# An attention and gated-MLP kernel: a second block's scores in pairs, and the lower halves of weights on another engine

## The chip, the cores and the metric

The kernel runs on one core of a Trainium2 chip. Its engines work side by side, each through its own queue of instructions: TensorE (PE; its weight loads are listed as PEld), VectorE (DVE), ScalarE (ACT), GpSimd (POOL) and SyncE (SP), which issues the DMAs. The metric is the device time in microseconds (us) of one execution.

## The reference

Local attention with a few global tokens, and a gated feed-forward layer behind it, all in float32:

```python
scores = scale * q @ k.T            # 4 batches, 8 heads, 768 tokens, head size 64
keep = (pos_k < 8) | ((rel >= 0) & (rel < 96))
a = softmax(where(keep, scores - slope[h] * dist, -1e9))
x = (a @ v), heads side by side     # 3072 tokens x 512
gate = 1 / (1 + exp(-(x @ w_gate)))            # 512 x 1536
out = (gate * (x @ w_val)) @ w_out             # 1536 x 512
```

## The kernel before, in words

**Tiles.** The 3072 tokens are cut into eight blocks of three tiles of 128 tokens (`TB`, `NB` = 384). Heads are taken in pairs, so a block has 4 pairs x 3 tiles = 12 items `(s, t)`. For an item the kernel computes the scores of both heads against a window of 256 keys (`WIN`: 96 before, 32 global slots, the 128 of the tile itself), adds a table of biases and takes the minimum of the negated row on VectorE (L406, in one instruction that also writes the minimum), the exponential with its sum on ScalarE (L419), the normalisation on VectorE (L438), the transposes (L452) and the product with v (L502). The result x of a block lies transposed, split into an upper half xh (rounded to the fast float form of TensorE) and a lower half xl, the remainder.

**Feed-forward.** The 1536 hidden columns are cut into 12 slices f. `ff_in` (L554) computes the gate (`ps_g`) and the value (`ps_u`) of a slice: for each, four chunks of 128 model columns times three products (w1l with xh, w1h with xl, w1h with xh). `ff_out` (L588) multiplies by the output slice and adds into three banks `ps_o`, again as three products with w2h and w2l. For the first six slices of the first block (`UNSPLIT`) the output slice is not split, and one product in full float32 stands in place of three. `ff_out` of a slice is issued after `ff_in` of the next one.

**Weights.** They arrive as 64 bit floats. Within the first block they are converted, in steps that `conv_step` (L241) advances: `conv_load` asks for the raw words two steps ahead; `conv_a` (L182) makes bits and exponent parts on ScalarE and VectorE; `conv_b` (L208) puts them together on VectorE; `conv_c` (L230) copies gate and value of a slice to the upper half w1h on ScalarE (128x1024) and takes the difference to the lower half w1l with two GpSimd subtractions of 128x512. w1h and w1l of all slices then stay in SBUF. The output slices stay unsplit as `w2f`; `split_w2` (L221, with `split`, L216) makes w2h on ScalarE and w2l on GpSimd anew for each slice and block, into one buffer each.

**Order of the work.** The first block's attention stands before everything else. The second block's attention (`PAIR` = 1) is spread over the twelve slices of the first block; later blocks' attention over the slices of the block before, with a split form and with transposes by DMA. A list of events gives each step its slice and one of four places in it (L632 to 654): 0 before `ff_in`, 1 between gate and value, 2 after `ff_in`, 3 after `ff_out`. For the second block an item's scores ("S") stood at place 0 of slice `k * 10 // 12`, its transposes ("T") at place 1 of the next slice, and the values ("V") of a pair of heads behind the last T. The third S of a pair of heads also asks for the loads of a later pair (`ready_step`, `load_step`, L289). Within this, a scheduler of the language orders the instructions of each engine by a model of their times and by priorities; `issue_after` (L62) fixes single places in the order without a wait.

**Banks.** The second block's scores used two PSUM banks, `ps_s` and `ps_v`, one for each head of an item, each holding 256 of 512 columns; the next item used the same two (`bank`, L351; `scores`, L359). The scores are matmuls in full float32 on half the rows of the array each, the second head's first (L371 to 378).

Of the kernel before, what the change touches and what calls it, by code (L numbers as in the profile page):

```python
# [8 lines left out]
F32 = mybir.dt.float32  # L9
# [6 lines left out]
ALU = mybir.AluOpType  # L16
# [3 lines left out]
P = 128  # L20
# [8 lines left out]
def attn_moe_kernel(ctx, tc, qT, kT, v, n_global, n_local, wg, wv, wo, out, B, H, S, D):  # L29
# [31 lines left out]

    def issue_after(later, earlier):  # L62
        tc.add_manual_dep(
            later.ins,
            earlier.ins.name,
            mybir.DependencyInfo(mybir.DependencyClass.NoSync, mybir.DependencyReason.DATA),
            reason="issue order",
        )
# [146 lines left out]

    def split(hi, lo, w):  # L216
        ins = nc.scalar.activation(hi, w, AF.Copy)  # L217
        sub(nc.gpsimd, lo, w, hi)
        return ins

    def split_w2(f, last=False):  # L221
        if last:
            hi, lo = (mpool.tile([P, DM], F32R, name="work", tag="work", bufs=WORKB) for _ in range(2))
        else:
            hi = w2pool.tile([P, DM], F32R, name="w2h")
            lo = w2pool.tile([P, DM], F32R, name="w2l")
        issue_after(split(hi, lo, w2f[f].bitcast(F32)), last_gate[-1])
        w2[0] = (f, hi, lo)

    def conv_c(j):  # L230
        c = conv[j]
        if c["i"] == 0:
            hi, lo = (t[c["f"]].rearrange("p i c n -> p (i c n)") for t in (w1h, w1l))
            w = c["bits"].bitcast(F32)
            nc.scalar.activation(hi, w, AF.Copy)
            for part in (slice(0, CW), slice(CW, 2 * CW)):
                sub(nc.gpsimd, lo[:, part], w[:, part], hi[:, part])
# [113 lines left out]
    def bank(*names):  # L351
# [5 lines left out]
        return pool.tile([P, 4 * P], F32, name=name)  # L357

    def scores(bi, s, t):  # L359
        b, t0, nt = blocks[bi]  # L360
# [5 lines left out]
        if bi <= PAIR:  # L366

            ps = [bank(*(("ps_s", "ps_g", "ps_u", "ps_o1") if bi < PAIR else ("ps_s", "ps_v"))) for _ in range(2)]

            lead = None  # L370
            for j in (1, 0):  # L371
                hd = slice(j * D, (j + 1) * D)
                ins = nc.tensor.matmul(
                    ps[j][:, :w], st["qr"][hd, 0, qc], st["kr"][hd, k0:k0 + w], start=True, stop=True
                )
                if lead is not None:
                    issue_after(ins, lead)
                lead = ins
            last_pe[:] = [lead]
            if (bi, s, t) == (0, 0, 1):  # L380
# [134 lines left out]
    def pair_out(bi, s, av, st):  # L515
# [3 lines left out]
        if bi < PAIR:  # L519
# [17 lines left out]
            x = mpool.tile([P, NB], F32, name="hh", tag="hh")  # L537
            nc.vector.tensor_tensor(x[:, :n], av[:, :n], rs[:, :n], op=ALU.mult)
            if s < NPAIR - 1:
# [14 lines left out]
    def ff_in(bi, f, mid=None):  # L554
# [4 lines left out]
        for i in range(2):  # L559
            ps = ps_gv.tile([P, NB], F32, name=("ps_g", "ps_u")[i])  # L560
            k = 0
            for c in range(NC):
                for wt, xt in ((w1l, xh), (w1h, xl), (w1h, xh)):
                    nc.tensor.matmul(  # L564
                        ps[:, :n], wt[f][:, i, c], xt[:, c, :n], start=(k == 0), stop=(k == 3 * NC - 1)
                    )
                    k += 1
            pss.append(ps)
            if i == 0:
                a = mpool.tile([P, NB], F32, name="work", tag="work", bufs=WORKB)  # L570
# [62 lines left out]
    for bi, (b, t0, nt) in enumerate(blocks):  # L633
# [5 lines left out]
        else:  # L639

            w = ((bi - 1) * NF - (LEAD + 1 if bi > PAIR + 1 else 0), bi * NF - LEAD - 1)
        for k, (s, t) in enumerate(items):
            u = w[0] + k * (w[1] - w[0]) // len(items)

# [5 lines left out]
            if t == nt - 1:  # L650
                after, kind = (2, 2) if bi < PAIR else (1, 1) if bi == PAIR else (2, 3)
                events.append((u + after * lag, kind, "V", bi, s, t))
# [51 lines left out]
    for u, (bi, f) in enumerate(seq):  # L704
# [36 lines left out]
        if bi >= PAIR or f >= UNSPLIT:  # L741
            split_w2(f, u == len(seq) - 1)
        prev = (bi, f)
# [152 lines left out]
```

## Time and profile before

| | us |
|---|---|
| median of 3 runs | 738.48 |
| lowest and highest | 736.40, 741.03 |
| the profiled execution | 736.18 |
| its span, first to last instruction | 734.4 |
| TensorE busy | 718.1 |
| VectorE busy | 498.8 |
| ScalarE busy | 420.2 |
| GpSimd busy | 219.4 |

The profile's times count from the span's start. A busy TensorE contains matmuls that overlap their neighbours, as they are pipelined; how fast it goes is read from the starts of one matmul and the next. "Idle before" names the instruction whose end released an engine after a wait.

### The profile page before, as it was taken

Reading aid. Unit: us, or ns where it says so; the run is one execution under the profiler, and the core shown is the slowest. Engines: PE = TensorE matmul, PEld = TensorE weight load, DVE = VectorE, ACT = ScalarE, POOL = GpSimd, SP = SyncE. Lnnn points to the kernel's source line nnn. Section 1 sums busy time; section 2 is a strip of 40 time slices with the busy share of each in tenths; the row PEclk is TensorE's granted clock in tenths of the full one; section 3 lists DMA queues with packets and bytes.
Section 4 is the critical chain, followed back from the end, with each engine's and each line's share of the span. In section 5 each row is a group of like instructions: output and inputs, shape, how many; then the busy total and the mean of one; then the engine's idle time right before and its main releaser. Section 6 shows DMA issues by size and latency. Waiting matters only on the chain. (4 is left out here: it accounts for less than half of the span.)

```text
span 734.4 us, 12477 instructions
## 1 busy us (share of the span) xinstructions
PE 718.1 (98%) x4403; PEld 653.0 (89%) x4403; DVE 498.8 (68%) x1303; ACT 420.2 (57%) x948; POOL 219.4 (30%) x166
## 2 busy tenths in 40 slices
PE   7999999999999999999999999999999999999996
PEld 5667788999889999999999999999999999999996
DVE  7889799668877777686777868666786877321111
ACT  5789887656565555566456655655555664332222
POOL 5424345422231323223132332313233231221222
PEclk9999999999999999999999999999999999999999
DMA  8969662624437353433435442343435224010001
GB/s 249 275 194 274 189 199 59 167 61 81 106 79 159 85 106 71 100 103 68 79 80 121 110 106 63 65 122 74 96 81 110 72 47 83 16 45 1 1 0 46
DMA packets 136866, 74.27 MB, mean 101 GB/s; under 512 B 87136, under 2 KB 129120, under 8 KB 136800
## 3 DMA queue, kind: packets, MB, share of 16 engines
q1 hardware_dynamic: 136800, 73.43, 40.1%
q8 instruction: 36, 0.59, 0.3%
q14 instruction: 30, 0.25, 0.1%
HBM read 49.81 MB, written 6.29 MB: 76 GB/s over the span
## 5 line engine op out<-in xcount | busy, mean ns | idle before, releaser
L180 POOL TENSOR_TENSOR w2l<-w2f,w2h 128x512 fp32r<-128x512 f32 x89 | 122.5, 1377 | 372.8 <-ACT w2h L217 359.1
L581 DVE SCALAR_TENSOR_TENSOR work<-work,ps_u 128x384 f32<-128x384 f32 x90 | 49.8, 553 | 127.1 <-PE ps_u L564 122.1
L564 PE MATMUL ps_g<-xh,w1l 128*128 128x384 f32 x384 | 131.1, 341 | 1.0 <-ACT work L572 1.0
L564 PE MATMUL ps_u<-xh,w1l 128*128 128x384 f32 x384 | 130.9, 341 | 0.1
L564 PE MATMUL ps_g<-xl,w1h 128*128 128x384 f32 x384 | 129.6, 337 | 0.7 <-DVE xl L545 0.7
L564 PE MATMUL ps_g<-xh,w1h 128*128 128x384 f32 x384 | 129.4, 337 | 0.0
L564 PE MATMUL ps_u<-xh,w1h 128*128 128x384 f32 x384 | 129.3, 337 | 0.0
L564 PE MATMUL ps_u<-xl,w1h 128*128 128x384 f32 x384 | 129.2, 336 | 0.0
L584 ACT ACTIVATE hh<-work 128x384 fp32r<-128x384 f32 x90 | 46.9, 521 | 131.3 <-DVE work L581 131.1
L419 ACT ACTIVATE work<-work,nms 128x256 f32<-128x256 f32 (+1 forms) x192 | 92.0, 481 | 25.8 <-DVE nms L406 25.4
L604 PE MATMUL ps_o<-w2l,hh 128*128 128x512 f32 x267 | 104.9, 393 | 0.6 <-POOL w2l L180 0.5
L604 PE MATMUL ps_o<-w2h,hh 128*128 128x512 f32 x267 | 104.1, 390 | 0.0
L604 PE MATMUL ps_o<-w2h,hl 128*128 128x512 f32 x267 | 103.1, 389 | 0.0
L180 DVE TENSOR_TENSOR hl<-work,hh 128x384 fp32r<-128x384 f32 x90 | 79.6, 884 | 23.4 <-ACT hh L584 23.2
L217 ACT ACTIVATE w2h<-w2f 128x512 fp32r<-128x512 f32 x89 | 56.0, 630 | 52.3 <-PE ps_o L604 51.0
L564 PEld LDWEIGHTS ps_g<-xh,w1l 128*128 128x128 f32 x384 | 72.2, 188 | 5.1 <-issue 2.3
L564 PEld LDWEIGHTS ps_u<-xh,w1l 128*128 128x128 f32 x384 | 72.1, 188 | 3.9 <-issue 1.2
L564 PEld LDWEIGHTS ps_g<-xl,w1h 128*128 128x128 f32 x384 | 72.2, 188 | 2.6 <-DVE xl L545 1.1
L564 PEld LDWEIGHTS ps_u<-xl,w1h 128*128 128x128 f32 x384 | 72.2, 188 | 1.0
L438 DVE TENSOR_SCALAR work<-work,rc 128x256 f32<-128x256 f32 (+1 forms) x168 | 71.4, 464 | 2.0
L564 PEld LDWEIGHTS ps_g<-xh,w1h 128*128 128x128 f32 x384 | 72.2, 188 | 0.5 <-issue 0.2
L564 PEld LDWEIGHTS ps_u<-xh,w1h 128*128 128x128 f32 x384 | 72.2, 188 | 0.0
(133 smaller groups left out, 1170.0 us busy)
## 6 DMA issues: line engine op xcount, KB each, us to landing
qr<-in_qT SPq DMA_DIRECT2D x56, 192.0 KB, 3.3
kr<-in_kT SPq DMA_DIRECT2D x32, 192.0 KB, 2.7
v<-in_v SPq DMA_DIRECT2D x32, 192.0 KB, 3.6
raw<-in_w_gate SPq DMA_DIRECT2D x12, 512.0 KB, 4.3
raw<-in_w_val SPq DMA_DIRECT2D x12, 512.0 KB, 5.6
raw<-in_w_out SPq DMA_DIRECT2D x12, 512.0 KB, 3.8
out<-ost SPq DMA_DIRECT2D x24, 256.0 KB, 2.2
v<-in_v SPq DMA_DIRECT2D x16, 144.0 KB, 3.8
```

What stands on the lines that cost most here:

```text
L180: eng.tensor_tensor(out, a, b, op=ALU.subtract)
L217: ins = nc.scalar.activation(hi, w, AF.Copy)
L419: ins = nc.scalar.activation(sb[:, j, :w], sb[:, j, :w], AF.Exp, scale=-1.0, bias=nm[:, j:j + 1], accum_out=sm[:, j:j + 1])
L438: nc.vector.tensor_scalar(sb[:, j, :w], sb[:, j, :w], rc[:, j:j + 1], None, op0=ALU.mult)
L564: nc.tensor.matmul(ps[:, :n], wt[f][:, i, c], xt[:, c, :n], start=(k == 0), stop=(k == 3 * NC - 1))
L581: nc.vector.scalar_tensor_tensor(a[:, :n], a[:, :n], 1.0, pss[1][:, :n], op0=ALU.add, op1=ALU.mult)
L584: nc.scalar.activation(hh[:, :n], a[:, :n], AF.Copy)
L604: ins = nc.tensor.matmul(outs[bi][t], ht[:, t * P:(t + 1) * P], wt, start=(f == 0 and k == 0), stop=(f == NF - 1 and k == len(parts) - 1),)
```

## The change

- `pair_scores` computes the scores of items into two banks. For the second block it takes two items: the first item's 256 columns lie in the left half of each bank, the second's in the right half. The matmuls are issued at a priority raised by 400, in their place behind the last feed-forward matmul written so far (`last_out`, which `ff_in` of the first block now notes too), and wait with a semaphore for the last minimum (`last_min`) and for the product of the first block's last pair of heads (`last_av`), which had the bank before.
- `twin_scores` is called by the first item of a pair and keeps the second's banks for its own call.
- The events of the second block are counted in quarters of a slice: both S of a pair at one place, every 6 or 7 quarters; T four quarters after S for the first item and six for the second; V one quarter after a pair of heads' last T.
- `conv_c` takes w1l of slices 1 to 11 with one VectorE subtraction of 128x1024 instead of two on GpSimd; slice 0 keeps them.
- `split` and `split_w2` get an engine: w2l of the first block (slices 6 to 11) goes to VectorE, the later blocks' stays on GpSimd.

```diff
-    def issue_after(later, earlier):
+    def issue_after(later, earlier, kind=mybir.DependencyClass.NoSync):
...
-    def split(hi, lo, w):
+    def split(hi, lo, w, eng):
         ins = nc.scalar.activation(hi, w, AF.Copy)
-        sub(nc.gpsimd, lo, w, hi)
+        sub(eng, lo, w, hi)
         return ins
...
             nc.scalar.activation(hi, w, AF.Copy)
+            if c["f"]:
+                sub(nc.vector, lo, w, hi)
+                return
             for part in (slice(0, CW), slice(CW, 2 * CW)):
                 sub(nc.gpsimd, lo[:, part], w[:, part], hi[:, part])
...
+    def pair_scores(bi, items):
+
+        names = ("ps_s", "ps_g", "ps_u", "ps_o1") if bi < PAIR else ("ps_s", "ps_v")
+        banks = [bank(*names) for _ in range(2)]
+        free = [] if bi < PAIR else [last_av[-1], last_min[-1]]
+        turn = [] if bi < PAIR else last_out[-1:]
+        lead = None
+        out = []
+        with tc.high_priority(offset=0 if bi < PAIR else 400):
+            for i, (s, t) in enumerate(items):
+                st = steps[bi, s]
+                w = P if blocks[bi][1] + t == 0 else WIN
+                qc = slice(t * P, (t + 1) * P)
+                k0 = t * SLOT + WIN - w
+                ps = [b[:, i * WIN:i * WIN + w] for b in banks]
+                for j in (1, 0):
+                    hd = slice(j * D, (j + 1) * D)
+                    ins = nc.tensor.matmul(ps[j], st["qr"][hd, 0, qc], st["kr"][hd, k0:k0 + w], start=True, stop=True)
+                    for before in free:
+                        issue_after(ins, before, mybir.DependencyClass.Sync)
+                    if bi < PAIR and lead is not None:
+                        issue_after(ins, lead)
+                    for before in turn:
+                        issue_after(ins, before)
+                    lead = ins
+                out.append(ps)
+        last_pe[:] = [lead]
+        return out
+
+    def twin_scores(bi, s, t):
+        nt = blocks[bi][2]
+        s2, t2 = divmod(s * nt + t + 1, nt)
+        ps, steps[bi, s2]["ps", t2] = pair_scores(bi, [(s, t), (s2, t2)])
+        return ps
...
+            ps = st.pop(("ps", t), None)
+            if ps is None:
+                ps = pair_scores(bi, [(s, t)])[0] if bi < PAIR else twin_scores(bi, s, t)
...
+            if bi < PAIR:
+                last_out[:] = [ins]
...
+            if bi == PAIR:
+                at = 4 * (k - k % 2) * w[1] // len(items)
+                turned = at + 4 + 2 * (k % 2)
+                events.append((*divmod(at, 4), "S", bi, s, t))
+                events.append((*divmod(turned, 4), "T", bi, s, t))
+                if t == nt - 1:
+                    events.append((*divmod(turned + 1, 4), "V", bi, s, t))
+                continue
...
-            split_w2(f, u == len(seq) - 1)
+            split_w2(f, u == len(seq) - 1, nc.vector if bi < PAIR else nc.gpsimd)
```

## Rows read from the trace of the kernel before

**Rows 1.** The page: busy tenths in 40 equal slices of the span.

```profile
PE   7999999999999999999999999999999999999996
...
DVE  7889799668877777686777868666786877321111
```

**Rows 2.** Busy us (instructions) in three stretches; then granted clock, DMA share, GB/s.

```profile
core 0: us, PE busy (x) PEld busy (x) DVE busy (x) ACT busy (x) POOL busy (x), PEclk, DMA share, GB/s
36.00:130.00 94.00, 91.33 (x510) 71.59 (x510) 83.50 (x160) 78.83 (x150) 39.50 (x27) 1.00 0.61 186
130.00:200.00 70.00, 68.18 (x423) 63.29 (x422) 50.84 (x155) 43.14 (x106) 22.44 (x15) 1.00 0.42 99
200.00:720.00 520.00, 519.92 (x3175) 487.96 (x3174) 334.51 (x882) 272.92 (x622) 136.43 (x93) 1.00 0.34 76
```

**Rows 3.** TensorE's timeline: start, us, instruction, count, [idle before <-releaser].

```profile
36.28 0.48 PE L373 MATMUL ps_v<-kr,qr 64*128 64x256 f32 x1
...
36.93 0.44 PE L564 MATMUL ps_g<-xh,w1l 128*128 128x384 f32 x1
...
38.28 0.44 PE L564 MATMUL ps_g<-xl,w1h 128*128 128x384 f32 x1 [0.74 <-DVE xl L545]
38.56 0.34 PE L564 MATMUL ps_g<-xh,w1h 128*128 128x384 f32 x1
38.74 0.34 PE L564 MATMUL ps_u<-xl,w1h 128*128 128x384 f32 x1
...
39.18 0.48 PE L373 MATMUL ps_v<-kr,qr 64*128 64x256 f32 x1
...
40.46 0.42 PE L564 MATMUL ps_g<-xh,w1l 128*128 128x384 f32 x1 [0.57 <-ACT work L572]
...
58.73 0.48 PE L373 MATMUL ps_v<-kr,qr 64*128 64x256 f32 x1 [0.84 <-DVE nms L406]
...
198.81 0.51 PE L387 MATMUL ps_s<-ks,qs 128*128 128x256 f32 x2 [1.20 <-DVE ks L180]
```

**Rows 4.** VectorE's groups from 36 to 130 us: busy us, mean ns | idle before.

```profile
L438 DVE TENSOR_SCALAR work<-work,rc 128x256 f32<-128x256 f32 x24 | 12.3, 551 | 0.2
L214 DVE SCALAR_TENSOR_TENSOR w2f<-top,w2f 128x512 int16<-128x512 int16 x11 | 11.9, 1085 | 1.9 <-ACT w2f L192 1.5
L206 DVE SCALAR_TENSOR_TENSOR top<-raw,neg 128x512 int16<-128x512 int16 x11 | 11.6, 1054 | 0.2
...
L180 DVE TENSOR_TENSOR hl<-work,hh 128x384 fp32r<-128x384 f32 x5 | 4.9, 988 | 0.6 <-ACT hh L584 0.6
...
L545 DVE TENSOR_TENSOR xl<-hh,xh 128x384 fp32r<-128x384 f32 x1 | 1.3, 1321 | 0.8 <-ACT xh L544 0.8
```

**Rows 5.** VectorE's timeline, single instructions: start, us, instruction.

```profile
42.05 0.68 DVE L206 SCALAR_TENSOR_TENSOR top<-raw,neg 128x512 int16<-128x512 int16 x1
...
42.84 0.74 DVE L214 SCALAR_TENSOR_TENSOR w2f<-top,w2f 128x512 int16<-128x512 int16 x1
...
43.65 0.35 DVE L438 TENSOR_SCALAR work<-work,rc 128x256 f32<-128x256 f32 x1
...
63.13 1.84 DVE L214 SCALAR_TENSOR_TENSOR w2f<-top,w2f 128x512 int16<-128x512 int16 x1
...
114.01 0.55 DVE L180 TENSOR_TENSOR hl<-work,hh 128x384 fp32r<-128x384 f32 x1
...
198.00 0.76 DVE L180 TENSOR_TENSOR ks<-kr,ks 64x576 fp32r<-64x576 f32 x1
```

**Rows 6.** Waits of SP's queue, 30 to 130 us: total, times, longest.

```profile
SPq L324 <- PE ps_t L502: 5.2, 2, 4.8
```

**Rows 7.** GpSimd's groups from 36 to 130 us, columns as in rows 4.

```profile
L180 POOL TENSOR_TENSOR w1l<-bits,w1h 128x512 fp32r<-128x512 f32 x22 | 31.7, 1461 | 40.6 <-ACT w1h L235 40.4
L180 POOL TENSOR_TENSOR w2l<-w2f,w2h 128x512 fp32r<-128x512 f32 x5 | 8.4, 1687 | 17.0 <-ACT w2h L217 10.4 <-ACT sm L432 6.5
```

**Rows 8.** GpSimd's timeline from 62 to 67 us.

```profile
63.05 3.02 POOL L180 TENSOR_TENSOR w1l<-bits,w1h 128x512 fp32r<-128x512 f32 x2 [3.93 <-ACT w1h L235]
```

**Rows 9.** ScalarE's copy to w1h, its group from 36 to 130 us.

```profile
L235 ACT ACTIVATE w1h<-bits 128x1024 fp32r<-128x1024 f32 x11 | 11.7, 1063 | 9.4 <-DVE bits L212 9.3
```

More of the change, by code (lines that the diff above doesn't have):

```diff
@@ L65, in issue_after @@
             earlier.ins.name,
-            mybir.DependencyInfo(mybir.DependencyClass.NoSync, mybir.DependencyReason.DATA),
+            mybir.DependencyInfo(kind, mybir.DependencyReason.DATA),
             reason="issue order",
@@ L214, in conv_b, with split_w2 @@
             nc.vector.scalar_tensor_tensor(top, c.pop("top"), 8.0, top, op0=ALU.mult, op1=ALU.add)
-    def split(hi, lo, w):
+    def split(hi, lo, w, eng):
         ins = nc.scalar.activation(hi, w, AF.Copy)
-        sub(nc.gpsimd, lo, w, hi)
+        sub(eng, lo, w, hi)
         return ins
-    def split_w2(f, last=False):
+    def split_w2(f, last=False, eng=nc.gpsimd):
         if last:
@@ L226, in split_w2 @@
             lo = w2pool.tile([P, DM], F32R, name="w2l")
-        issue_after(split(hi, lo, w2f[f].bitcast(F32)), last_gate[-1])
+        issue_after(split(hi, lo, w2f[f].bitcast(F32), eng), last_gate[-1])
         w2[0] = (f, hi, lo)
@@ L357, in bank @@
         return pool.tile([P, 4 * P], F32, name=name)
+    last_av = []
+    def pair_scores(bi, items):
[30 more added lines that the diff above has]
+        return ps
     def scores(bi, s, t):
@@ L366, in scores @@
         if bi <= PAIR:
[L368 to L379, printed above, removed]
+            ps = st.pop(("ps", t), None)
+            if ps is None:
+                ps = pair_scores(bi, [(s, t)])[0] if bi < PAIR else twin_scores(bi, s, t)
             if (bi, s, t) == (0, 0, 1):
@@ L537, in pair_out @@
             x = mpool.tile([P, NB], F32, name="hh", tag="hh")
-            nc.vector.tensor_tensor(x[:, :n], av[:, :n], rs[:, :n], op=ALU.mult)
+            last_av[:] = [nc.vector.tensor_tensor(x[:, :n], av[:, :n], rs[:, :n], op=ALU.mult)]
             if s < NPAIR - 1:
@@ L563, in ff_in @@
                 for wt, xt in ((w1l, xh), (w1h, xl), (w1h, xh)):
-                    nc.tensor.matmul(
+                    ins = nc.tensor.matmul(
                         ps[:, :n], wt[f][:, i, c], xt[:, c, :n], start=(k == 0), stop=(k == 3 * NC - 1)
@@ L650, in attn_moe_kernel @@
             if t == nt - 1:
-                after, kind = (2, 2) if bi < PAIR else (1, 1) if bi == PAIR else (2, 3)
+                after, kind = (2, 2) if bi < PAIR else (2, 3)
                 events.append((u + after * lag, kind, "V", bi, s, t))
```

## The prediction

> **What bounds the kernel now.** First the page's slices [rows 1]: TensorE's digit is 9 in all of them but the first and the last, while VectorE stands at 7 to 9 only in the first third and at 6 to 7 later. Then the stretches that the change touches [rows 2]. From 36 to 130 us (the first block's slices, with the second block's attention between them) TensorE is busy for 91.33 of 94.00 us, so 2.67 us pass without a matmul; from 130 to 200 us 1.82 us; in the 520 us after that 0.08. The granted clock is 1.00 in all three, the 2.4 GHz level. So the time is the sum of what TensorE has to do plus small holes. Whoever wants to gain has to close holes before 200 us (4.5 us in these two stretches) or take TensorE work away; whoever loses has to open new ones. VectorE, with 83.50 of 94.00 us, has 10.5 us free in the first block's stretch, less than any engine but TensorE.
>
> Third, the order of TensorE's instructions with what ended its holes [rows 3]. At 36.28 us stand the first item's scores, then a gate matmul; 0.74 us of hole in front of 38.28 wait for xl, the lower half of the first block's activations, from VectorE. At 39.18 come the second item's scores; 0.57 us in front of 40.46 wait for ScalarE's tanh. In front of the scores at 58.73 lie 0.84 us, which wait for VectorE's minimum of the item before: their bank was still to be read. These three are 2.15 of the 2.67 us.
>
> The profiled execution took 736.18 us: 734.4 of span and 1.78 around it. The median of the runs shown is 738.48, 2.30 above. I do the sums on 736.18 and add 2.30 at the end.
>
> **The change part by part.**
>
> *Scores in pairs.* The 24 score matmuls stay; only their places change. An item's scores take 0.65 us of TensorE's order (36.28 to 36.93 [rows 3]), so a second item right behind the first costs the same again. What a group of scores costs beside that is the return: the first gate matmul behind a hole or a change of form takes 0.28 us to the next start (38.28 to 38.56), the one after it 0.18 (38.56 to 38.74). Six groups fewer save 6 x 0.10 = 0.6 us. That transposes which now stand beside scores lose this neighbour can eat it: bounds 0 and 0.6; I take 0.6, since transposes and scores of other pairs also come to stand together.
>
> The second gain is the wait for the bank. Before, both banks belong to one item, and the next item comes less than a slice later; this cost 0.84 us at 58.73. Now a pair comes every 1.5 to 1.75 slices, some 13 us at 94 us for about twelve slices, and four minima have to be taken in that time. The hole goes: 0.84 us. The new wait (semaphores of the last minimum and of the product of the first block's last pair) holds what is behind the scores on TensorE's queue, which is the next gate or output matmuls, and with them all that reads these banks; with 13 us of room I price it at nothing. Its bounds: nothing, and 0.84 us for each of the six pairs, 5.0 us, if VectorE lags each time as it did once.
>
> The third is the start. The second item's scores now stand behind the first's, at about 36.9 us, in front of a gate that waits for xl until 38.28 in any case. So their 0.65 us fall into the hole of 0.74, and the separate group at 39.18 goes. Besides, that xl took 1321 ns [rows 4] where the same form took 0.55 us later [rows 5], beside a GpSimd subtraction that now goes away. Either closes the hole; both together don't give it twice: 0.74 us. The 0.57 us in front of 40.46 wait for ScalarE, which nothing here speeds up: they stay.
>
> Transposes come a slice or one and a half after their scores, values a quarter later; each keeps at least the slack it had, so 0. The loads of q, k and v for a later pair of heads hang on a third item's scores and move by two or three quarters of a slice either way. They stand on SP's queue in front of weight loads, and the load of v waits there until the values before it have been computed: 4.8 us at the longest now [rows 6]. Two of these waits grow by two quarters, some 4 us. I take 0, since the weights are asked for two steps ahead of their use; bounds 0 and 8 us, both uncovered.
>
> The dependency kind, the note of the last input matmul and the priority of 400 issue no instruction; they only fix the places counted above: 0.
>
> *Lower halves on VectorE.* Removed from GpSimd: 22 subtractions of 128x512 for w1l, 1461 ns each, and six for w2l (five of them in this stretch), 1687 ns each [rows 7]. Slice 0 keeps its two. GpSimd was busy for 39.50 of 94.00 us [rows 2], so its relief by itself is worth nothing. Added on VectorE: 11 subtractions of 128x1024 and 6 of 128x512. No row of before has that form with 1024 columns. Undisturbed, 384 columns took 0.55 us and 576 took 0.76 [rows 5], 1.09 ns a column; hence an estimate of 1.25 us for 1024 and 0.69 for 512, together 13.8 + 4.1 = 17.9 us, 17.2 of them before 130 us. Bounds: 1024 columns can't take less than the 0.55 us of 384, and at the rate of the disturbed 384 (1321 ns) they would take 3.5; I take the undisturbed rate, since the disturber goes.
>
> Given back: VectorE's instructions that run beside GpSimd's subtractions are held up. The write of w2f took 1.84 us at 63.13, where GpSimd's two ran from 63.05 [rows 8], and 0.74 us at 42.84 without them [rows 5]. Group means [rows 4] against undisturbed rows [rows 5]: normalisation 24 x (551 - 350) ns = 4.8 us; w2f 11 x (1085 - 740) = 3.8; top 11 x (1054 - 680) = 4.1; hl 5 x (988 - 550) = 2.2. Together 14.9 us. So VectorE goes from 83.5 to 83.5 + 17.2 - 14.9 = 85.8 of 94 us, still below TensorE. The edit trades one delay for another of nearly the same size, and TensorE sees nothing of it: 0. The cover is the 8.2 us left free.
>
> The new waits: each subtraction now stands in VectorE's queue behind ScalarE's copy to the upper half, 1063 ns [rows 9]. Minima, gate products and the bits of later slices queue behind it, and ScalarE in turn waits for those bits (9.3 us already in this stretch [rows 9]). Bounds: nothing, where the copy is done by then, and 17 x 1.06 = 18.0 us of VectorE standing still. I take none on TensorE; the 8.2 us carry nearly half of the upper bound. If they don't suffice, the next to be late is the bank of the scores, then w1l itself, which a gate needs within a slice.
>
> Sum: 0.84 + 0.74 + 0.6 = 2.2 us less; 736.2 becomes 734.0, and on the median's scale 736.3.
>
> **The rivals.** *VectorE becomes the bound (slower).* Place: 36 to 130 us. If the time of the held-up instructions doesn't come back, because VectorE would have stood waiting for ScalarE there anyway, its load is 83.5 + 17.2 = 100.7 in a stretch of 94, 6.7 us too much, with the sixth w2l 7.4: 743.6, or 745.9 on the median's scale. It decides from the point where less than 6.7 of the 14.9 us come back. For it: 10.5 us is little room, and ScalarE and VectorE wait for each other [rows 9]. Against it: 1.84 against 0.74 us is a delay of a running instruction, not of a waiting one.
>
> The Trainium skill speaks for this rival: "Perfetto Trace Analysis", section Optimizing Scalar/DVE Operations, says that with a saturated VectorE it may pay to offload work to ScalarE or even GpSimd, and this change goes the other way. The same place warns that moving work between VectorE and GpSimd might not help, since they share a port; with that half the trace agrees (1.84 against 0.74 us [rows 5, 8]), and for the first no row shows whether 83.5 of 94 us is saturation.
>
> *All holes close (faster).* If the new order has no waits at all up to 200 us, 2.67 + 1.82 us go, with the 0.6: 736.2 - 5.1 = 731.1, or 733.4. Against it: the largest hole after 130 us, 1.20 us at 198.81, waits for ks [rows 3], which nothing here touches.
>
> *The pairing does nothing.* What is written is a priority, and the rest of the order is the scheduler's: if waits as long as those removed appear elsewhere, the time stays at 736.2, or 738.5. For it: the room on VectorE hardly changes. Against it: the hole at 58.73 has its cause in the sharing of the banks alone.
>
> **How the numbers follow.** Forecast 0.54 (736.3), nothing 0.23 (738.5), slower 0.16 (745.9, a milder form of it 3 to 6 us over before), all holes 0.07 (733.4). The runs of before spread from 736.4 to 741.0, so a median can be off by some 2 us. The range of 731.5 to 742.5 holds all but the full form of the slower rival, and of the open bounds (5.0 us at the banks, 8 us at SP's queue) about half. One per cent, 7.4 us, is about what a measurement of this kernel can tell from no change: faster by more 0.04 (more than the closing of all holes), within it 0.85, slower 0.11.
>
> **What would show it.** Right: from 36 to 130 us the score matmuls come in six groups of two items with no hole over 0.3 us in front of one; the gate at 38 us starts without 0.74 us of waiting; the 128x1024 subtraction takes about 1.25 us on VectorE, w2f and top are back to 0.74 and 0.68 us in the mean, and VectorE's busy time in this stretch is near 86 us. Wrong: VectorE's subtractions come behind long waits for w1h, TensorE's holes in the stretch sum to more than 5 us, or the first block's last slice ends later than before.

## The result, and the profile after

The change takes 742.32 us, median of 22 runs (741.01 to 747.07, and one of 794.71), beside 738.60 us of the kernel before in 22 runs on the same chips (735.26 to 741.63). The ratio is 1.0067 [1.0049, 1.0084], with the 95% interval in brackets: it is slower, by 5 us on 738 (the two medians lie 3.7 us apart). All ratios below are to the kernel before on the same chip; they leave out the single runs that took far longer than the rest (this one, and one of 1825.6 us in each of e10 and e12).

The profiled execution took 744.60 us (span 742.8), 8.4 more than that of before. The page's slices, which answer to [rows 1]:

```profile
PE   8999998999989999999999999999999999999996
```

TensorE has two 8s behind its first slice, the seventh (111 to 130 us) and the twelfth (204 to 223). The stretches, to be laid beside [rows 2], and two short ones (columns as there):

```profile
36.00:130.00 94.00, 88.19 (x506) 70.43 (x505) 78.67 (x174) 77.17 (x146) 0.00 (x0) 0.98 0.59 191
130.00:200.00 70.00, 67.59 (x419) 62.77 (x418) 50.01 (x147) 41.12 (x102) 16.84 (x11) 1.00 0.44 103
200.00:720.00 520.00, 517.90 (x3165) 486.12 (x3164) 338.96 (x893) 274.77 (x628) 137.56 (x94) 1.00 0.34 77
...
118.00:120.20 2.20, 0.02 (x1) 0.02 (x1) 2.20 (x7) 2.20 (x5) 0.00 (x0) 1.00 0.00 0
121.00:124.00 3.00, 3.00 (x9) 2.25 (x8) 2.33 (x4) 0.68 (x1) 0.00 (x0) 0.50 0.46 175
```

From 36 to 130 us 5.81 us pass without a matmul, 2.67 before; behind 130 us 4.51, before 1.90. VectorE is less busy than before, and GpSimd not at all until 130 us. From 118 to 120.2 us TensorE stands still while VectorE and ScalarE work without a break; behind it the granted clock is 0.50, the 1.2 GHz level. TensorE's waits from 36 to 138 us (total, times, longest):

```profile
PE ps_o L636 <- DVE w2l L180: 2.3, 1, 2.3
PE ps_g L594 <- ACT work L604: 1.7, 2, 1.3
...
PE ps_g L594 <- DVE xl L575: 0.3, 1, 0.3
```

The longest is one wait for the lower half w2l; two are for a tanh.

And TensorE's timeline, which answers to [rows 3]: the first pair of items, and the long hole.

```profile
39.12 0.48 PE L381 MATMUL ps_v<-kr,qr 64*128 64x256 f32 x1
...
40.19 0.44 PE L594 MATMUL ps_g<-xh,w1l 128*128 128x384 f32 x1
...
41.10 0.45 PE L594 MATMUL ps_g<-xl,w1h 128*128 128x384 f32 x1 [0.30 <-DVE xl L575]
...
120.18 0.49 PE L636 MATMUL ps_o<-w2l,hh 128*128 128x512 f32 x1 [2.27 <-DVE w2l L180]
...
121.30 0.63 PE L636 MATMUL ps_o<-w2l,hh 128*128 128x512 f32 x1
121.73 0.63 PE L636 MATMUL ps_o<-w2h,hh 128*128 128x512 f32 x1
```

Two items take 1.07 us of the order (39.12 to 40.19), where one took 0.65 before. The scores stand in six groups of two items, and no hole stands in front of any of them. The output matmuls behind the long hole start 0.43 us apart instead of 0.23.

**An account of the 8.4 us.** I cut the span at two places: the first gate matmul of the second slice (40.46 us before [rows 3], 42.45 after) and the first of the third block (224.46 and 232.42). Ahead of the first cut the change loses 2.0 us: its first block's attention ran at half clock from 11.35 to 21.59 us in this execution, which single executions of other kernels below show too and others don't, and the change doesn't touch that work. Three kernels below with the same order up to this cut (e3, e5, e7) ran there at full clock and reached it at 40.13, 38.95 and 38.83 us: at equal clock the change is 0.3 to 1.6 us ahead of 40.46, not behind. Behind the second cut the two differ by 0.4 us. Between the cuts the change is 6.0 us longer (190.0 against 184.0). With the 0.4 and the lead at the start, 4.8 to 6.1 us remain, which fits the 5 us of the ratio. TensorE's holes there sum to 9.15 us, against 3.27; half clock lasts 3.41 us, against none, and costs about half of that, 1.7 (the spacing of 0.43 against 0.23). What is left is TensorE's own order: 179.1, against 180.7. So 5.9 + 1.7 - 1.6 = 6.0. The same account of one profiled execution each, in us:

```
kernel                      between the cuts   holes   half clock/2   rest
before                           184.0          3.3        0.0       180.7
the change                       190.0          9.2        1.7       179.1
e1 pairs alone                   195.8         12.4        3.4       180.0
e2 VectorE alone                 188.1          5.8        1.7       180.6
e6 second item later             190.2          7.5        3.4       179.3
e13 the same, items singly       188.8          5.9        1.7       181.2
e14 conversion behind hh         189.4          8.6        1.7       179.1
e16 behind hh and w2h            192.8          9.6        3.4       179.8
```

In the profiled executions of all kernels here the rest is 180.3 to 181.2 where the second block's scores stand singly, and 178.8 to 180.3 where they stand in pairs: the pairs save TensorE about 1.2 us in the mean.

VectorE's groups from 36 to 138 us, by which the stretch's end has moved (busy us, mean ns | idle before), answer to [rows 4]:

```profile
L180 DVE TENSOR_TENSOR w1l<-bits,w1h 128x1024 fp32r<-128x1024 f32 x11 | 13.4, 1220 | 0.7 <-ACT w1h L235 0.6
L214 DVE SCALAR_TENSOR_TENSOR w2f<-top,w2f 128x512 int16<-128x512 int16 x11 | 8.3, 751 | 0.9 <-ACT w2f L192 0.6
L180 DVE TENSOR_TENSOR top<-top,neg 128x1024 int16<-128x1024 int16 x11 | 8.0, 730 | 9.8 <-ACT neg L199 7.5 <-ACT top L199 2.1
...
L180 DVE TENSOR_TENSOR w2l<-w2f,w2h 128x512 fp32r<-128x512 f32 x5 | 3.5, 691 | 1.4 <-ACT w2h L217 1.4
```

The new subtractions take what was reckoned (1220 and 691 ns) and hardly wait for their copies (0.7 and 1.4 us in all). What VectorE now waits for is ScalarE's conversion, 9.8 us in front of `top`. That leads to ScalarE.

**Why w2l is late at 118 us.** ScalarE's timeline after:

```profile
110.27 0.51 ACT L449 ACTIVATE work<-work,nms 128x256 f32<-128x256 f32 x1 [0.48 <-DVE nms L436]
...
111.77 0.49 ACT L449 ACTIVATE work<-work,nms 128x256 f32<-128x256 f32 x1
...
112.26 1.12 ACT L192 ACTIVATE bits<-raw 128x1024 int32<-128x1024 uint32 x1
113.28 1.12 ACT L199 ACTIVATE top<-raw 128x1024 int16<-128x1024 int16 x1
114.30 1.12 ACT L199 ACTIVATE neg<-raw 128x1024 int16<-128x1024 int16 x1
115.33 0.65 ACT L192 ACTIVATE w2f<-raw 128x512 int32<-128x512 uint32 x1
...
115.97 1.14 ACT L192 ACTIVATE bits<-raw 128x1024 int32<-128x1024 uint32 x1
117.01 0.52 ACT L616 ACTIVATE hh<-work 128x384 fp32r<-128x384 f32 x1
...
117.51 0.62 ACT L217 ACTIVATE w2h<-w2f 128x512 fp32r<-128x512 f32 x1
```

and VectorE's in the same time:

```profile
111.12 0.56 DVE L613 SCALAR_TENSOR_TENSOR work<-work,ps_u 128x384 f32<-128x384 f32 x1
115.46 0.69 DVE L180 TENSOR_TENSOR top<-top,neg 128x1024 int16<-128x1024 int16 x1 [3.78 <-ACT neg L199]
...
118.29 0.57 DVE L180 TENSOR_TENSOR hl<-work,hh 128x384 fp32r<-128x384 f32 x1
...
118.83 0.70 DVE L206 SCALAR_TENSOR_TENSOR top<-raw,neg 128x512 int16<-128x512 int16 x1
119.42 0.71 DVE L180 TENSOR_TENSOR w2l<-w2f,w2h 128x512 fp32r<-128x512 f32 x1
```

The product that hh copies is done at 111.68 us, but hh starts at 117.01, 5.3 us later: four exponentials stand in one piece, five conversion steps behind them, and hh behind those. w2h follows and is done at 118.13. Then VectorE's queue adds 1.3 us: w2l stands there behind a normalisation, the remainder hl, which had to wait for hh too, and a conversion step, and starts at 119.42. TensorE waits until 120.18. In ScalarE's timeline before, the same slice has two exponentials and two steps:

```profile
110.76 0.49 ACT L419 ACTIVATE work<-work,nms 128x256 f32<-128x256 f32 x1
...
111.75 0.65 ACT L192 ACTIVATE w2f<-raw 128x512 int32<-128x512 uint32 x1
112.31 1.17 ACT L192 ACTIVATE bits<-raw 128x1024 int32<-128x1024 uint32 x1
113.37 0.52 ACT L584 ACTIVATE hh<-work 128x384 fp32r<-128x384 f32 x1
113.78 0.63 ACT L217 ACTIVATE w2h<-w2f 128x512 fp32r<-128x512 f32 x1
```

There hh starts 3.2 us after its product (110.2), w2l comes from GpSimd, and the hole in front of the output matmul is short:

```profile
116.40 0.50 PE L604 MATMUL ps_o<-w2l,hh 128*128 128x512 f32 x1 [0.32 <-POOL w2l L180]
```

The Trainium skill, "PSUM — Partial Sum Buffer", section Engine vs sequencer instructions, says that ScalarE's, VectorE's and GpSimd's queues are strictly first in, first out; this trace agrees: hh had its input for 5.3 us and passed none of the steps ahead of it.

### The profile page after: what moved, and what is told of

The parts are those of the page before. It is cut to its first block, busy times and chain, and to the rows that moved or that the text cites. A ratio compares the mean times of both kernels' runs of the same rounds, so it can differ in the third digit from the quotient of the medians.

```text
span 742.8 us, 12440 instructions
## 1 busy us (share of the span) xinstructions
PE 722.2 (97%) x4403; PEld 657.7 (89%) x4403; DVE 497.2 (67%) x1320; ACT 420.1 (57%) x948; POOL 176.7 (24%) x138
## 5 line engine op out<-in xcount | busy, mean ns | idle before, releaser
L180 POOL TENSOR_TENSOR w2l<-w2f,w2h 128x512 fp32r<-128x512 f32 x83 | 112.1, 1351 | 356.9 <-ACT w2h L217 349.8
L180 DVE TENSOR_TENSOR hl<-work,hh 128x384 fp32r<-128x384 f32 x90 | 75.4, 837 | 22.9 <-ACT hh L616 22.8
L180 POOL TENSOR_TENSOR qs<-qr,qs 128x768 fp32r<-128x768 f32 x24 | 44.9, 1872 | 178.3 <-DMA qr<-in_qT 101.8
L497 DVE COPY halves<-work 128x512 int16<-128x512 int16 (+1 forms) x144 | 62.6, 477 | 16.4 <-DMA turned<-halves 14.9
```

The costliest lines, as they stand in the source:

```text
L180: eng.tensor_tensor(out, a, b, op=ALU.subtract)
L497: nc.vector.tensor_copy(dst, words[:, :, :, h])
```

## The experiments

### The two halves, alone and in part

**e1_pairs**: the change with all lower halves on GpSimd as before.

```diff
-            if c["f"]:
-                sub(nc.vector, lo, w, hi)
-                return
...
-            split_w2(f, u == len(seq) - 1, nc.vector if bi < PAIR else nc.gpsimd)
+            split_w2(f, u == len(seq) - 1)
```

> The pairs of scores alone, all lower halves on GpSimd again. Theory A (the four exponentials of a pair stand together on ScalarE and push the copies hh and w2h back, so that the first block's output matmuls wait): the loss stays, ratio to before about 1.005 (742 us), with a hole of 1 us or more in front of an output matmul between 100 and 130 us and a stretch at half the granted clock behind it. Theory B (the subtractions in VectorE's queue come late): the loss is gone and the closed bank hole remains, ratio 0.997 to 1.000 (736.5 to 738.5 us).

Measured: 749.91 us, 1.0171 [1.0139, 1.0203]. **e2_engines**: the kernel before with the two hunks on lower halves alone.

> The lower halves on VectorE alone, scores item by item as before. Theory A: no loss, ratio 0.998 to 1.001. Theory B: ratio about 1.005 (742 us), with TensorE waiting for w2l or w1l from VectorE for 1 us or more at least once.

Measured: 740.13 us, 1.0038 [1.0022, 1.0054]. **e3_w2_back** and **e4_w1_back**: the change with the second, or the first, of the hunks of e1 alone.

> The change with w2l of the first block back on GpSimd. If the 2.27 us that an output matmul waited for w2l at 118 us come from VectorE's queue, they shrink below 0.7 us, the clock stays at 1.00 behind them and the time falls by 3 to 4 us to about 738.5 (ratio 1.000). Under theory A the hole stays above 1.5 us, for w2h comes as late as before, and the ratio stays at 1.004 to 1.007.

> The change with w1l back on GpSimd, w2l of the first block on VectorE. Theory B in the form that w1l's 1.25 us on VectorE cause the delays: ratio 0.997 to 1.001. Theory A, or w2l alone as the cause: ratio 1.004 to 1.007. GpSimd's subtractions hold VectorE up again, so its busy time in the first block's stretch rises by some 10 us against the change.

Measured: 743.37 us, 1.0095 [1.0063, 1.0126], and 745.28 us, 1.0122 [1.0092, 1.0152].

The halves don't add. The pairs alone lose 1.7%. The engine edit alone loses 0.4%, but beside the pairs it wins back 1.0 points (1.0171 to 1.0067): 0.8 if only w1l moves (e3), 0.5 if only w2l moves (e4). The wait for w2l near 118 us stays in both: 1.68 us in e3, from GpSimd, and 1.83 in e4, from VectorE. Pairs alone wait in TensorE's order for GpSimd, in e1 from 36 to 140 us:

```profile
PE ps_g L591 <- POOL w1l L180: 2.8, 3, 1.9
PE ps_o L633 <- POOL w2l L180: 2.6, 1, 2.6
```

So both lower halves come late with the pairs, on whichever engine they are taken, and VectorE, more than twice as fast at it (1220 ns for what took GpSimd 2 x 1461 [rows 7]), shortens the wait. With the pairs, the move to VectorE isn't the cause of the loss.

### What makes them late

Four theories: the priority of 400 puts the scores too early; hh has too low a priority; the two items' exponentials come in one piece; the conversion steps stand in front of hh.

**e7_no_priority** and **e5_hh_first**:

```diff
-        with tc.high_priority(offset=0 if bi < PAIR else 400):
+        with tc.high_priority(offset=0):
```

```diff
-        nc.scalar.activation(hh[:, :n], a[:, :n], AF.Copy)
-        sub(nc.vector, hl[:, :n], a[:, :n], hh[:, :n])
+        with tc.high_priority(offset=400 if bi < PAIR else 0):
+            nc.scalar.activation(hh[:, :n], a[:, :n], AF.Copy)
+            sub(nc.vector, hl[:, :n], a[:, :n], hh[:, :n])
```

> The change without the raised priority of the pairs' matmuls. Theory A: the pair still brings its four exponentials at once, ratio 1.004 to 1.009. Rival C in the form that the priority puts scores in front of feed-forward matmuls which ScalarE and VectorE wait for: ratio 0.998 to 1.002.

> The change, with the first block's copy hh and remainder hl raised in priority as the scores are. Theory A1 (hh comes late on ScalarE behind a pair's exponentials and the weight conversion, and w2l behind it): the 2.27 us in front of an output matmul at 118 us shrink below 0.7 us, no half clock behind them, time 3 to 4 us below the change (ratio to before about 1.002). Rival A2 (all of ScalarE's queue is late by a pair's work, whatever stands first): the delay moves to a gate or to w1l, and the ratio stays at 1.005 to 1.009.

Measured: 742.91 us, 1.0058 [1.0037, 1.0078], and 742.50 us, 1.0067 [1.0042, 1.0092]. Without the pairs' priority the loss stays, so it isn't the cause. In e5 the order on ScalarE stayed as it was, and a hole of 2.12 us stands at 114.5, so e5 didn't try its theory.

**e6_second_later**: the second item of a pair keeps its place on TensorE, but its minima and exponentials come three quarters of a slice later. **e13_single_new_list**: the same list of events, with each item's scores at its own place.

```diff
-                events.append((*divmod(at, 4), "S", bi, s, t))
+                events.append((*divmod(at + 3 * (k % 2), 4), "S", bi, s, t))
```

```diff
-                ps = pair_scores(bi, [(s, t)])[0] if bi < PAIR else twin_scores(bi, s, t)
+                ps = pair_scores(bi, [(s, t)])[0]
```

> The change, with the second item's minima and exponentials three quarters of a slice later; its matmuls still stand with the first item's. Theory A (four minima and four exponentials of a pair in one piece make the queues of VectorE and ScalarE late): the holes of TensorE between 40 and 140 us fall from 5 us to about 2, ratio 1.000 to 1.003. Rival C (the places of transposes, values and loads in the new list of events, or the priority, make the delay): holes and ratio stay as in the change, 1.005 to 1.009.

> As the run with the second item three quarters later, but each item's scores are computed by themselves at its own place (no pairing of matmuls left; list of events, priority and engines as there). If the pairing of the matmuls itself costs or gives something, this differs from that run (1.0034) by more than 0.002; theory A says that the matmuls' place is worth at most 0.84 us and that the ratio lies within 1.002 to 1.005.

Measured: 740.88 us, 1.0034 [1.0019, 1.0049], and 743.65 us, 1.0067 [1.0043, 1.0091]. Taking the four exponentials apart gives back about half of the loss. The same list with single scores is 0.33 points slower than with pairs, some 2 us, with intervals that just overlap; the column of the rest agrees (181.2 against 179.3). The whole stretch doesn't show it in the two profiled executions (188.8 and 190.2), where e6 has longer holes and one half clock more.

e13 also bears on the cause. It has neither paired matmuls nor four exponentials in one piece, its waits from 36 to 140 us sum to 2.8 us, and it still loses as much as the change: in its profile a hole of 1.82 us at 166 us, with half clock behind it, stands in the second block. So the exponentials in one piece are not the whole of the loss. e6 keeps waits of another kind, here from 36 to 140 us:

```profile
PE ps_g L594 <- DVE w1l L180: 2.4, 2, 1.6
```

**e14_conv_behind_hh**: the change, with each conversion's first step on ScalarE ordered behind the last hh. **e16_conv_behind_w2**: behind the last w2h too, whose split is issued ahead of the conversion (second diff). **e15_later_behind_hh** and **e17_later_behind_w2**: these two with e6's line.

```diff
         if last_exp:
             issue_after(first, last_exp[-1])
+        if last_hh:
+            issue_after(first, last_hh[-1])
...
-        nc.scalar.activation(hh[:, :n], a[:, :n], AF.Copy)
+        last_hh[:] = [nc.scalar.activation(hh[:, :n], a[:, :n], AF.Copy)]
```

```diff
+        if bi >= PAIR or f >= UNSPLIT:
+            last_hh[:] = [split_w2(f, u == len(seq) - 1, nc.vector if bi < PAIR else nc.gpsimd)]
         if bi < PAIR:
             conv_until(2 * f + 1)
-        if bi >= PAIR or f >= UNSPLIT:
-            split_w2(f, u == len(seq) - 1, nc.vector if bi < PAIR else nc.gpsimd)
```

> The change, with each later step of the weight conversion on ScalarE placed behind the last hh written. In front of the hh at 117 us stand four exponentials and five conversion operations (5 us); this takes two of them (bits and w2f, 1.8 us) away. Theory A (ScalarE's queue order makes the 2.27 us hole): the hole falls to 0.5 us or less and the half clock behind it goes, ratio 1.002 to 1.004. Rival (w2l's and hl's place in VectorE's queue makes it): the hole stays near 2 us, ratio 1.006 to 1.007.

> The change, with the conversion steps of the first block's split slices placed behind hh and w2h of the slice, so that these stand right behind the exponentials on ScalarE. Theory A: no output matmul of the first block waits over 0.5 us, ratio 1.000 to 1.003; the conversion comes later by 1 to 2 us, and if its own slack is used up, gates wait for w1l instead (A2) and the ratio stays at 1.005 or more.

> The change with both: the second item's minima and exponentials three quarters of a slice later, and later conversion steps on ScalarE behind hh. If they cure different waits: ratio 0.999 to 1.002, holes from 40 to 140 us below 3 us. If both move the same waiting of one full queue: 1.003 to 1.005.

> As the run before it, with the second item's minima and exponentials three quarters of a slice later. If the two act independently this is the best version of the change: ratio 0.998 to 1.001. If both only move the same waiting, 1.003 to 1.005.

Measured: e14 740.78 us, 1.0042 [1.0025, 1.0059]; e16 746.08, 1.0091 [1.0057, 1.0125]; e15 742.05, 1.0073 [1.0051, 1.0094]; e17 745.83, 1.0091 [1.0060, 1.0121]. TensorE's waits from 36 to 140 us, the longest in total, in e14 and then in e16:

```profile
PE ps_t L485 <- ACT pT L490: 1.9, 2, 1.2
...
PE ps_o L639 <- DVE w2l L181: 0.8, 1, 0.8
```

```profile
PE ps_g L599 <- DVE w1l L181: 2.9, 4, 1.9
```

With hh ahead of the next steps the hole at 118 us shrinks from 2.27 to 0.81 us, and a new one of 1.23 us comes at 121.8, where transposes wait for a copy on ScalarE. w2h starts no earlier in e14 (117.62 us); hl does, by 2.1 us, and w2l then starts at 118.35, almost at once behind w2h. So hh's place on ScalarE acts here through VectorE's queue. With w2h ahead too, that hole is gone, and the gates wait for w1l, whose conversion has been put back. e17 again has a hole of 2.87 us in front of the output matmuls. e6 takes back half of the loss and e14 over a third, though e14's interval overlaps the change's; both together (e15) give nothing. So the chain raw, bits, w1h, w1l and the chain product, hh, w2h, w2l share ScalarE, and in these runs whichever went first made the other late. That the holes of the first block follow the order on ScalarE is shown; an order in which both chains are in time wasn't found, and the half of the loss that e6 leaves isn't explained by one cause.

### What the engine edit costs in the second block

e2 has no hole over 0.14 us from 41 to 130 us, and its first block is even shorter: from the first cut to the first gate of the second block it takes 84.1 us, against 85.2 before. Its loss lies at 160 to 170 us. GpSimd's, VectorE's and TensorE's timelines of e2:

```profile
161.52 1.92 POOL L180 TENSOR_TENSOR qs<-qr,qs 128x768 fp32r<-128x768 f32 x1 [6.47 <-ACT qs L348]
```

```profile
161.81 3.74 DVE L180 TENSOR_TENSOR ks<-kr,ks 64x448 fp32r<-64x448 f32 x2
```

```profile
161.88 0.44 PE L567 MATMUL ps_g<-xh,w1l 128*128 128x384 f32 x1 [1.82 <-ACT work L575]
...
166.19 0.44 PE L567 MATMUL ps_u<-xh,w1l 128*128 128x384 f32 x1 [1.97 <-DVE work L584]
```

Two things have moved, though no line of this block was edited. First, the scores of one item of the third block stand behind six of the nine output matmuls of a slice, ahead of all nine in the kernel before; ScalarE's copies of k and q follow the scores, the tanh follows the copies, and the gate waits 1.82 us (0.47 before). The change has this too, and its ScalarE shows the chain:

```profile
167.38 1.18 ACT L346 ACTIVATE ks<-kr 64x448 fp32r<-64x448 f32 x2 [2.57 <-PE ps_s L417]
168.58 0.84 ACT L348 ACTIVATE qs<-qr 128x768 fp32r<-128x768 f32 x1
169.33 0.47 ACT L604 ACTIVATE work<-ps_g 128x384 f32<-128x384 f32 x1
```

Second, GpSimd's subtraction of q starts 0.29 us ahead of VectorE's two of k, which then take 3.74 us. Before, VectorE's started first, and took a third:

```profile
161.46 1.27 DVE L180 TENSOR_TENSOR ks<-kr,ks 64x448 fp32r<-64x448 f32 x2
```

The Trainium skill, "SBUF — State Buffer", section Who interferes with whom, says that a VectorE instruction with two inputs in SBUF contends with a GpSimd instruction that reads SBUF, and that the order of issue decides who is blocked; the trace agrees, 3.74 against 1.27 us. The product behind them is late, hence the 1.97 us, and half clock follows for 3.41 us from 166.97. The change doesn't have this second meeting.

**e8_engines_wait**: e2, where q's subtraction waits with a semaphore for k's. **e9_before_wait**: the same edit on the kernel before, for what it costs by itself.

```diff
-            sub(nc.vector, ks[o, j, w], kr[a, w], ks[a, j, w])
+            low = sub(nc.vector, ks[o, j, w], kr[a, w], ks[a, j, w])
...
-        sub(nc.gpsimd, qs[:, :, 1, :n], qr[:, :, :n], qs[:, :, 0, :n])
+        issue_after(sub(nc.gpsimd, qs[:, :, 1, :n], qr[:, :, :n], qs[:, :, 0, :n]), low, mybir.DependencyClass.Sync)
```

> The lower halves on VectorE alone (scores item by item), and GpSimd's subtraction for q in the later blocks waits for VectorE's subtractions for k of the same pair of heads. Theory D (in the run of the lower halves alone, the loss comes from one place at 164 us, where GpSimd's subtraction for q starts 0.3 us before VectorE's for k and holds it up to 3.74 us, and a stretch at half clock follows): the k pair takes 1.3 us, the 1.97 us hole and the half clock are gone, the time falls by 3 to 4 us to a ratio of 0.998 to 1.000. Rival: the order of the second block is at fault whatever the ports do, ratio stays at 1.003 to 1.005.

> The kernel before, with GpSimd's subtraction for q in the later blocks waiting for VectorE's for k. If the meeting costs the kernel before its 1.20 us hole at 198 us: ratio 0.997 to 0.999, faster than both kernels. If the wait only moves the delay to the q side, as in the run of the lower halves with this wait (2.4 us hole at 209 us): 1.000 to 1.003.

Measured: 740.44 us, 1.0023 [1.0006, 1.0040], and 741.52 us, 1.0062 [1.0043, 1.0080]. The meeting is gone in e8, and the old order of the scores came back by itself, but scores at 211.0 now wait 2.42 us for a minimum. On the kernel before the same wait makes a hole of 2.35 us near 206 us and half clock behind it, 4.8 us by the medians (741.52 - 736.76), with nothing of the change in it.

**e10_engines_order**, **e11_change_order**, **e12_later_order**: e2, the change and e6, with that one item's scores put back in front of all nine output matmuls.

```diff
+            last_scores[:] = [ins]
...
+                if (bi, f) == (PAIR, 2) and k == 0:
+                    issue_after(ins, last_scores[-1])
```

> The lower halves on VectorE alone, with one place of the second block's order put back to what it is in the kernel before: the scores of the sixth item of the third block stand in front of all nine output matmuls instead of behind six. Theory E (these scores hold ScalarE's copies of k, and with them the next tanh, so that a gate stands 1.82 us in the late place and 0.47 us in the early one): the hole falls to about 0.5 us, the half clock that follows it is gone, and the time falls by 1.3 to 3 us to a ratio of 0.999 to 1.002. Rival: something else makes up the loss of 1.0038, ratio stays at 1.003 to 1.005.

> The change with the same place put back. Theory E: the 1.82 us hole at 168 us falls to about 0.5 us, ratio from 1.0067 to 1.003 to 1.005, what stays being the holes of the first block. Rival: nothing moves, ratio 1.006 to 1.008.

> The change with the second item's minima and exponentials three quarters of a slice later, and the same place put back. If the losses of the bunched exponentials and of this place are independent, both go: ratio 0.999 to 1.002 (737.5 to 739.7 us). If only one of them is real, 1.002 to 1.004.

Measured: 741.21 us, 1.0037 [1.0020, 1.0054]; 742.84, 1.0071 [1.0052, 1.0089]; 740.35, 1.0031 [1.0016, 1.0045]. In each the gate's hole falls from 1.82 to 0.47 us, and none differs from the same kernel without the edit by more than its interval: in e10 2.42 us of waiting for the product stay at the value matmuls behind it, with half clock. So neither the order nor the meeting could be taken out to win back e2's 0.4%: each repair leaves or opens another wait in the same block. How much of the loss belongs to which stays open.

### What a hole costs beyond itself

**e18_made_hole**: the kernel before, with sixteen copies on ScalarE ahead of one tanh in the fifth block; tanh overwrites what they write.

```diff
+                for _ in range(16 if (bi, f) == (4, 6) else 0):
+                    nc.scalar.activation(a[:, :n], ps[:, :n], AF.Copy)
```

> The kernel before with 16 more copies on ScalarE in front of one tanh of the fifth block, which make one hole of about 2.4 us on TensorE where it has none. If a hole costs its own length, the ratio is 1.003 (2.4 us). If a stretch at half clock follows it each time, 1.7 us come on top: ratio 1.0055.

Measured: 746.18 us, 1.0126 [1.0095, 1.0156]. The hole came out at 6.68 us, much longer than those of the change, so it says nothing of how short a hole may be. The stretches of the hole and behind it:

```profile
447.00:451.00 4.00, 0.00 (x0) 0.00 (x0) 1.79 (x4) 3.84 (x7) 1.88 (x1) 0.98 0.22 56
451.00:454.00 3.00, 0.35 (x1) 0.35 (x2) 0.37 (x1) 2.85 (x6) 0.00 (x0) 0.50 0.43 123
454.00:458.00 4.00, 4.00 (x14) 4.00 (x14) 1.86 (x3) 1.29 (x4) 1.29 (x1) 0.54 0.46 77
```

The clock falls inside the hole and stays at half until 457.66, 4.0 us into the work behind it; half of that, 2.0 us, is the price beside the 6.68, together 8.7 us. The ratio gives 9.3, with an interval of 7.0 to 11.5, so it agrees with that price and doesn't prove it. This is how I price the half clock in the account above.

## Why the prediction was wrong

The forecast was 736.3 us; the change takes 742.3, slower than before where a small gain was forecast.

**The step that failed** is the price of nothing for the new waits on TensorE. It stands twice: in "Scores in pairs" ("with 13 us of room I price it at nothing") and in "The new waits" ("I take none on TensorE"). For the pairs I counted the four minima on VectorE and not the four exponentials on ScalarE; this part fails by itself, as e1 shows (1.0171). For the lower halves I reckoned the room on VectorE (8.2 us free) and asked whether each has to wait for its own copy. It hardly does (0.7 and 1.4 us). What I didn't follow is the queue of ScalarE: a pair brings four exponentials in one piece and draws the conversion steps behind them, and hh, w2h, tanh and pT come behind these. I wrote down that ScalarE and VectorE wait for each other [rows 9], and drew no price from it. The pairs' bounds (5.0 us at the banks) were for another place: in front of the scores there is no hole at all. The holes went to output matmuls, gates and transposes. This term was 0, and measures 5.9 us of holes and 1.7 of half clock; the latter had no place in my sum. Of the 5.9 us, 2.6 lie behind 130 us, in a block that I took as untouched; why its order moves stays open.

**What was right.** The hole in front of the first xl fell from 0.74 to 0.30 us, and for the reason given: the second item's scores stand in front of that gate and cover 0.42 us of it (1.07 - 0.65). With pairs and the slow subtraction (e1), and with single scores and the fast one (e2), the gate waits:

```profile
37.94 0.44 PE L591 MATMUL ps_g<-xl,w1h 128*128 128x384 f32 x1 [0.33 <-DVE xl L572]
```

```profile
37.95 0.44 PE L567 MATMUL ps_g<-xl,w1h 128*128 128x384 f32 x1 [0.69 <-DVE xl L548]
```

So "Either closes the hole" was wrong: the faster subtraction (550 ns instead of 1321) closes almost nothing, since on VectorE xl now comes behind a w1l subtraction. The returns were taken too low: I counted 0.6 us for all, and TensorE's order between the cuts got 1.6 us shorter in the change and 1.9 between e13 and e6, of which the shorter place of two items gives 6 x (2 x 0.65 - 1.07) = 1.4. The subtraction of 1024 columns takes 1220 ns (forecast 1250), that of 512 takes 691 (690). The give-back came in full: w2f 751 ns, `top` 689, the normalisation 351, hl 557.

**Gone, but not for the reason given.** The hole at 58.73 is gone, but not by the sharing of the banks alone, as I wrote: e2 shares them as before and has no hole there either. The minimum that the scores waited for stood behind two normalisations, which ran beside GpSimd's subtractions (56.54 to 59.12 us) in the kernel before and with GpSimd at rest in e2:

```profile
56.28 1.71 DVE L438 TENSOR_SCALAR work<-work,rc 128x256 f32<-128x256 f32 x2
```

```profile
55.45 0.60 DVE L441 TENSOR_SCALAR work<-work,rc 128x256 f32<-128x256 f32 x2
```

In e9 and e18, whose first block is that of the kernel before, the same two took 2.70 and 2.67 us, and the hole was 1.86 and 1.83 us. Either half of the change removes it.

**The rivals.** VectorE became no bound: it is busy 78.67 of the 94 us from 36 to 130, less than before and less than the 86 forecast, and stands waiting for ScalarE. The advice of the Trainium skill, "Perfetto Trace Analysis", section Optimizing Scalar/DVE Operations, to relieve a saturated VectorE didn't bear here: with the pairs, taking the lower halves back to GpSimd costs 1.0 points (e1). "The pairing does nothing" named the right mechanism, waits that appear elsewhere, but stopped at equal size. "All holes close" fell. The transfers on SP's queue: the waits of loads behind values grew from 5.2 [rows 6] to 8.7 us (30 to 138 us), as bounded; the wait for a transfer of w2f's raw words grew on ScalarE from 0.4 to 4.5 us (36 to 130 us). The longest of these (2.29 us) ends at 123.13, behind the long hole, and from 104.5 to 120 us ScalarE waits for no transfer; so transfers didn't make that hole directly, and whether they had a part in ScalarE's order wasn't tried.

Of the signs set for it, "TensorE's holes in the stretch sum to more than 5 us" came true (5.81), and so did the later end of the first block's last slice (the second block's first gate starts at 131.42 us, before at 125.61, and 2.0 us of that were lost ahead of the first cut); "long waits for w1h" didn't.

## What to carry to other kernels

Work put together for one engine comes together on the next one too: before pairing scores, follow the four exponentials through ScalarE's queue and name what stands behind them and who waits for that. Room on an engine is not room in its queue. And with an order made by a scheduler, an edit in one block may move the order in a later one: measure the parts of a change alone and together, since here one part costs 0.4% alone and gains 1.0 points in company, and a hole that both parts close is counted once.

## What the runs showed of the hardware

A hole of about 2 us cost nearly double in some places. In these profiles half clock (0.50, the 1.2 GHz level) lasted 3.41 us behind holes of 2.27 (the change), 1.97 (e2), 2.35 (e9), 2.42 (e10), 2.87 (e17), 1.88 (e16), 1.62 (e6) and 1.54 us (e7); with TensorE at work throughout, about half of it, 1.7 us, is lost. It didn't follow each such hole: none came behind 2.54 us in e4 or 2.42 us in e8. The same hole of 1.82 us in front of one gate of the second block drew it in e5, e6, e7, e13, e14, e16 and e17, and not in e1, e3, e15 and the change. Which holes draw it wasn't settled here.

VectorE's instructions took longer beside GpSimd's subtractions, by amounts that differ between executions: the same two normalisations took 1.71, 2.70 and 2.67 us in the kernel before, e9 and e18, and 0.60 us in e2, where GpSimd stood still.
